# The query weights of a one-token attention block, loaded by eight transfers of sixteen partitions each

## The chip, the core and the metric

The kernel runs on one core of a Trainium2 chip. Its time is the device time of one execution in microseconds; the figure for the kernel before is the median of three runs. The core has five engines with instruction streams of their own: TensorE (PE; PEld is its weight load), VectorE (DVE), ScalarE (ACT), GpSimd (POOL) and SyncE (SP). SP does no arithmetic here: it issues DMA transfers, and sixteen DMA engines carry them out. Data lie in HBM (outside the core) and in SBUF, the core's own buffer of 128 partitions. TensorE adds up into PSUM.

## The reference

One token for each of two sequences is normalised, projected to 32 query heads, attends to a cache of 32768 keys and values for each of 8 key heads, and is projected back. The result is multiplied by the SiLU of a small gated MLP of the token itself and added to the token. All numbers are float32.

```
x, D = A_x, 512                                  # 2 x 1 x 512
xn = layernorm(x)
q = xn @ wq                                      # 512 x 4096: 32 heads of 128
scores = q . k_cache * 128**-0.5                 # k_cache 2 x 8 x 32768 x 128, 4 query heads share one
o = softmax(scores) . v_cache
s = o @ wo                                       # 4096 x 512
gate = x @ W_gate ; gate = gate * (gate > 0)     # 512 x 1792, as W_up
g = silu((gate * (x @ W_up)) @ W_down)
out = x + s * g
```

## The kernel before

**What is loaded.** The two caches are 256 MiB each (2 x 8 x 32768 x 128 x 4 bytes), the query weights `wq` 8 MiB, `wo` 8 MiB, the three MLP matrices 3.5 MiB each. Every byte is read once, so the kernel is above all a stream of DMA transfers.

**Buffers.** There are three large tiles in SBUF, each 128 partitions by 16384 floats (64 KiB a partition, 8 MiB in all): two for keys (`k0`, `k1`, in Python `kbuf`) and one, `wide` (shown as `w` in the profile), which holds first `wq`, then the gate and up weights, then the down weights, and then the values, a load at a time. The output weights `wo` go into `k1` at the end.

**How a load is written.** Every helper call records an operation with the tiles that it reads and writes; a small planner (`Program`) turns these into semaphore waits. `load(dst, src, sem, w=[...])` records one DMA on SP's queue whose completion adds 16 to the semaphore `sem`. The row of `wide` with number p takes four whole rows of `wq`, which lie one behind the other in HBM: 64 KiB in one piece. The load of `wq` is the first thing that SP issues:

```
QW = wq.shape[1] // 2
wqt = wide.rearrange("p (k h n) -> p k h n", k=NKC, h=2)
load(wide, wq.rearrange("(p k) n -> p (k n)", k=NKC), "wq", w=["wide"])
```

**The order of the work.** The order is that of the Python code; there is no scheduler. `load_kk(0)` (the first keys) follows the load of `wq` on SP. Then `project_q` multiplies the normalised token `xn`, which lies in `wt0`, by all of `wq` in 32 written matmuls (64 in the profile, since a float32 matmul is run in two passes). Its first matmul waits for the semaphore `wq`, that is, for the whole of `wq`, and for DVE's copy of `xn`:

```
for half in range(2):
    pe(chain([mm(pq[half][32 * c : 32 * c + 32, :], xn[:, k, :],
                 wqt[:, k, half, c * 512 : (c + 1) * 512], k == 0, k == NKC - 1)
              for k in range(NKC) for c in range(4)]),
       ["wt0", "wide"], [f"m{half}"])
```

`load_gu` overwrites `wide` with the gate and up weights, so SP waits for these matmuls before it issues it, and `load_kk(1)` stands behind that on SP. After this the 64 tiles of the caches (8192 tokens each) are worked through in pairs, in a loop `for j in range(PAIRS + 2)`: DVE turns the keys of a pair in 32 x 32 blocks (`k_transpose`, line 660 of the profile), TensorE makes the scores (`s`), DVE takes them out and keeps their maximum, ACT takes the exponential once a group of four tiles is complete, TensorE lays the weights out again (`pt`), DVE turns them (`wt`), and TensorE multiplies them by the values (`o`). SP issues the load of a pair's values into `wide` as soon as TensorE has finished with the values before, and the load of the next keys right behind it. The token itself, `x`, comes by two small transfers on ACT's queue, and DVE and ACT make `xn` of it while `wq` is on its way.

The profile gives the line 243 for every matmul recorded by the helper `mm`, and 240 for every transfer recorded by `load`.

Of the kernel before, what the change touches and what calls it, by code (L numbers as in the profile page):

```python
# [8 lines left out]
P = 128  # L9
# [6 lines left out]
ALIGN = 512  # L16
PERIOD = 4
APART = 16


class Op:
# [141 lines left out]
def decode_block_kernel(nc, x, kc, vc, wq, wo, wg, wu, wd, out):  # L163
# [8 lines left out]
    NKC = D // P  # L172
# [8 lines left out]
    def sbuf(name, *shape, align=32):  # L181
        return nc.alloc_sbuf_tensor(name, list(shape), F32, align_bytes=align)[:]
# [5 lines left out]
    wide = sbuf("w", P, 2 * NC * NR * DH, align=ALIGN)  # L188
# [41 lines left out]
    def dve(fn, r=(), w=()):  # L230
        pg.op("DVE", fn, r, w)
# [4 lines left out]
    def pe(fn, r=(), w=()):  # L236
        pg.op("PE", fn, r, w)

    def load(dst, src, sem, r=(), w=(), engine="SP"):
        pg.op(engine, lambda e: e.dma_start(dst, src), r, w, dma=sem)  # L240

    def mm(out_, lhs, rhs, start, stop):
        return lambda e: e.matmul(out_, lhs, rhs, start=start, stop=stop, skip_group_check=True)  # L243

    def chain(parts):
        def emit(e):
            for f in parts:
                got = f(e)
            return got

        return emit
# [6 lines left out]

    QW = wq.shape[1] // 2
    wqt = wide.rearrange("p (k h n) -> p k h n", k=NKC, h=2)  # L260
    load(wide, wq.rearrange("(p k) n -> p (k n)", k=NKC), "wq", w=["wide"])

    def of_columns(t):
        return t[0:P:APART, :]

    def by_column(t):
        return t.rearrange("b s (c n) -> c (b s) n", c=4)
# [20 lines left out]
    dve(lambda e: e.memset(xy, 0.0), w=["xy"])  # L288
    load(xp[0 : B * APART : APART, :], x.rearrange("b s d -> (b s) d"), "xp", w=["st0"], engine="ACT")
    load(of_columns(xy), by_column(x), "xy", w=["xy"], engine="ACT")  # L290
# [6 lines left out]
    for kb in range(4):  # L297
        dve(
            lambda e, kb=kb: e.memset(block_of[Q * kb : Q * kb + Q, kb * REP : (kb + 1) * REP], 1.0),
            w=["block_of"],  # L300
# [27 lines left out]
    n = 1  # L328
    while n < Q:
# [18 lines left out]
    dve(  # L348
        lambda e: e.tensor_copy(both, ident.rearrange("p (c k) -> p k c", c=NC)[:, 0 : B * APART : APART, :]),
        ["ident"],  # L350
# [40 lines left out]
                lambda e, k=k: e.transpose(  # L391
                    px[:, k * 32 : (k + 1) * 32], xquad[:, k, :], ident[:32, :32]
                )
# [62 lines left out]
    def project_q():  # L456
        pq = ps_m
        for half in range(2):
            pe(
                chain(  # L460
                    [
                        mm(
                            pq[half][32 * c : 32 * c + 32, :],
                            xn[:, k, :],
                            wqt[:, k, half, c * 512 : (c + 1) * 512],
                            k == 0,
                            k == NKC - 1,
                        )
                        for k in range(NKC)
                        for c in range(4)  # L470
                    ]
                ),
                ["wt0", "wide"],
                [f"m{half}"],
            )
        pt = ps_p[0]
        nq = REP * B * HKV
        turned = pt[:, :nq].rearrange("p (h b k) -> p h b k", h=REP, b=B)
        for half in range(2):
            qs = os_[half]  # L480
            dve(lambda e, q=qs, h=half: e.tensor_copy(q, pq[h]), [f"m{half}"], [f"os{half}"])  # L481
            pe(
                chain(
                    [
                        mm(
                            turned[:, h, :, half * NC : (half + 1) * NC],
                            qs[:, h * DH : (h + 1) * DH],
                            both,
                            True,
                            True,  # L490
                        )
                        for h in range(REP)
                    ]
                ),
                [f"os{half}", "both"],
                ["pt0"],
            )
        dve(lambda e: e.tensor_copy(qd.rearrange("p h b k -> p (h b k)"), pt[:, :nq]), ["pt0"], ["qd"])
        pq2 = ps_p[1]
        pe(  # L500
            chain(
                [
                    mm(
                        pq2[:, i * nq : (i + 1) * nq],
                        spread[:, i].rearrange("p k l -> p (k l)"),
                        qd.rearrange("p h b k -> p (h b k)"),
                        True,
                        True,
                    )
                    for i in range(4)  # L510
                ]
            ),
            ["st3", "qd"],
            ["pt1"],
        )
        dve(
            lambda e: e.tensor_copy(
                qall.rearrange("p b k e h -> p (b k) e h"),
                pq2[:, : 4 * nq].rearrange("p (e h g) -> p g e h", e=4, h=REP),
            ),  # L520
            ["pt1"],
            ["qall"],
        )
        take_query(0)

    def take_query(g):
        b, hk = group(g)
        pg.op(
            "POOL",
            lambda e: e.tensor_tensor(  # L530
                qcur.rearrange("p e (k h) -> p e k h", h=REP),
                qall[:, b, hk].unsqueeze(2).to_broadcast([P, 4, Q // REP, REP]),
                block_of.rearrange("p (k h) -> p k h", h=REP)
                .unsqueeze(1)
                .to_broadcast([P, 4, Q // REP, REP]),
                op=ALU.mult,
            ),
            ["qall", "block_of"],
            ["qcur", "pool"],
        )  # L540
# [243 lines left out]
    def finish_group(g):  # L784
# [27 lines left out]
            lambda e: e.tensor_copy(  # L812
                ots[mine, hk // 4, :, b * APART],
                ot[mine].rearrange("p (j m) -> p j m", j=ROWS)[:, :, 0],
# [61 lines left out]

    load_kk(0)
    project_q()
    load_gu()
    load_kk(1)  # L880
# [115 lines left out]
```

## Time and profile before

| | |
|---|---|
| time, median of 3 runs | 1309.93 us (1309.86 to 1310.05) |
| the profiled execution's own time | 1310.29 us |
| its span, first to last instruction | 1308.4 us |
| mean granted TensorE clock | 0.828 |
| PE busy | 859.0 us (66% of the span) |
| DVE busy | 718.1 us (55%) |
| ACT busy | 51.4 us (4%) |
| POOL busy | 10.5 us (1%) |
| SP's DMA queue, share of 16 DMA engines | 99.7% |
| read from HBM | 564.67 MB, 432 GB/s over the span |

The profile is of one execution, 0.36 us above the median of the runs. A busy share tells how long an engine had something under way; which engine sets the end is read from who waits for whom. Times in the answers are counted from the start of the span.

### The profile page before, as it was taken

What the parts mean: (1) busy time and instruction counts of PE and PEld (TensorE: products, weight loads), DVE (VectorE), ACT (ScalarE), POOL (GpSimd) and SP (SyncE); (2) the same over time, 40 slices, a digit from 0 to 9 for tenths busy, and PEclk for the clock granted to TensorE, in tenths of its full rate; (3) what the DMA queues carried; (4) which work ended last, traced back from release to release, by engine and by line L of the source; (5) the groups of instructions that cost most, each with busy time, mean ns of one, the idle gap of its engine ahead of it and who ended that gap; (6) DMA issues with size and microseconds to landing.
All of it is one profiled execution on the core that took longest, in us unless ns stands there. A gap on an engine that the chain in (4) does not pass through costs nothing.

```text
span 1308.4 us, 11146 instructions
## 1 busy us (share of the span) xinstructions
PE 859.0 (66%) x4720; PEld 211.5 (16%) x4720; DVE 718.1 (55%) x690; ACT 51.4 (4%) x133; POOL 10.5 (1%) x38
## 2 busy tenths in 40 slices
PE   3566675785666587576667667667665757865676
PEld 1111111211111121111111112121111112111121
DVE  3566654565655456664546666455665545656521
ACT  0001000000000000000000000000000000000000
POOL 0000000000000000000000000000000000000000
PEclk9677788878878887878898778798887889788788
DMA  9999999999999999999999999999999999999998
GB/s 417 423 438 435 437 431 441 425 439 429 437 429 439 435 433 441 429 441 427 439 429 437 429 439 435 433 441 429 441 427 439 429 437 429 439 435 433 439 431 357
DMA packets 10693, 564.79 MB, mean 432 GB/s; under 512 B 1195, under 2 KB 1211, under 8 KB 1597
## 3 DMA queue, kind: packets, MB, share of 16 engines
q1 hardware_dynamic: 10668, 564.67, 99.7%
q8 instruction: 6, 0.10, 0.0%
q14 instruction: 3, 0.02, 0.0%
q10 hardware_dynamic: 16, 0.01, 0.0%
HBM read 564.67 MB, written 0.00 MB: 432 GB/s over the span
## 4 chain that ended last, share of the span: by engine, by line
DMA 64%; DVE 17%; PE 15%; issue 4%; SPq 0%
DMA k<-in_A_k_cache_dram 58%; DVE k L660 17%; PE o L243 8%; PE s L243 6%; DMA k<-in_A_wo_dram 3%; DMA w<-in_A_wq_dram 2%; PE m_ps L243 1%; PE m_ps L693 0%; PE d L243 0%; SPq L240 0%; DVE gy L870 0%; DVE gy L872 0%
## 5 line engine op out<-in xcount | busy, mean ns | idle before, releaser
L243 PE MATMUL s<-k,qcur 128*32 128x512 f32 x2048 | 504.5, 710 | 370.5 <-DVE k L660 370.3
L660 DVE STREAM_TRANSPOSE k<-k 128x2048 f32<-128x2048 f32 x256 | 565.2, 2275 | 147.0 <-DMA k<-in_A_k_cache_dram 147.0
L243 PE MATMUL o<-w,wt 128*16 128x512 f32 x1984 | 245.5, 596 | 9.0 <-DMA w<-in_A_v_cache_dram 9.0
L243 PEld LDWEIGHTS s<-k,qcur 128*32 128x32 f32 x2048 | 89.5, 123 | 785.0 <-DVE k L660 639.3
L737 DVE STREAM_TRANSPOSE wt<-pt 128x512 f32<-128x512 f32 x64 | 45.9, 717 | 139.4 <-PE pt L243 134.6
L678 DVE TENSOR_SCALAR_CACHE_REDUCE st<-s 128x512 f32<-128x512 f32 x64 | 43.0, 672 | 120.9 <-PE s L243 120.9
L243 PEld LDWEIGHTS o<-w,wt 128*16 128x16 f32 x1984 | 62.4, 98 | 167.5 <-issue 167.5
L722 ACT ACTIVATE st<-st,nb 128x512 f32<-128x512 f32 x64 | 45.4, 710 | 1111.0 <-DVE nb L719 1111.0
L243 PE MATMUL pt<-st,perm 128*128 128x512 f32 x128 | 72.6, 696 | 1.5 <-ACT st L722 1.5
L763 DVE RECIPROCAL rl<-m_ps 128x1 f32<-128x1 f32 x16 | 2.7, 169 | 111.0 <-PE m_ps L243 111.0
L243 PE MATMUL m_ps<-ob,heads 128*128 128x128 f32 x128 | 21.7, 321 | 29.0 <-DVE ob L777 29.0
L243 PEld LDWEIGHTS pt<-st,perm 128*128 128x128 f32 x128 | 25.3, 219 | 34.4 <-issue 30.1
L803 DVE STREAM_TRANSPOSE os<-m_ps 128x512 f32<-128x512 f32 x16 | 11.5, 717 | 23.2 <-PE m_ps L243 23.2
L243 PEld LDWEIGHTS m_ps<-ob,heads 128*128 128x128 f32 x128 | 18.0, 217 | 31.1 <-DVE ob L777 31.1
L243 PE MATMUL m_ps<-w,wt 128*32 128x512 f32 (+1 forms) x128 | 16.2, 640 | 8.1 <-DMA w<-in_A_wq_dram 8.1
L777 DVE SCALAR_TENSOR_TENSOR ob<-o,share,ob 128x128 f32<-128x128 f32 x48 | 16.9, 351 | 1.7
L530 POOL TENSOR_TENSOR qcur<-qall,block_of 128x128 f32<-128x128 f32 x16 | 6.5, 406 | 1008.3 <-PE s L243 974.0
L243 PE MATMUL m_ps<-negone,mrow 1*128 1x1 f32 x32 | 6.0, 256 | 9.3 <-DVE mrow L708 9.3
L722 ACT ACTIVATION_READ_ACCUMULATOR st<-st,nb 128x1 f32 x64 | 11.9, 186 | 0.0
L481 DVE COPY os<-m_ps 128x512 f32<-128x512 f32 x2 | 1.4, 692 | 16.3 <-PE m_ps L243 16.3
L243 PE MATMUL o<-k,wt 128*16 128x512 f32 x64 | 8.4, 687 | 2.8 <-DMA k<-in_A_v_cache_dram 2.8
L391 PE MATMUL m_ps<-ident,st 32*128 32x32 f32 x4 | 0.7, 307 | 14.0 <-DVE st L380 14.0
(80 smaller groups left out, 102.8 us busy)
## 6 DMA issues: line engine op xcount, KB each, us to landing
k<-in_A_wo_dram SPq DMA_DIRECT2D x1, 4096.0 KB, 37.3
w<-in_B_W_gate_dram SPq DMA_DIRECT2D x1, 3584.0 KB, 19.6
w<-in_B_W_up_dram SPq DMA_DIRECT2D x1, 3584.0 KB, 27.6
w<-in_B_W_down_dram SPq DMA_DIRECT2D x1, 3584.0 KB, 15.6
k<-in_A_wo_dram SPq DMA_DIRECT2D x1, 2048.0 KB, 41.7
k<-in_A_wo_dram SPq DMA_DIRECT2D x1, 1024.0 KB, 43.7
k<-in_A_k_cache_dram SPq DMA_DIRECT2D x32, 48.2
k<-in_A_wo_dram SPq DMA_DIRECT2D x1, 512.0 KB, 44.5
```

What stands on the lines that cost most here:

```text
L243: return lambda e: e.matmul(out_, lhs, rhs, start=start, stop=stop, skip_group_check=True)
L391: lambda e, k=k: e.transpose(px[:, k * 32 : (k + 1) * 32], xquad[:, k, :], ident[:32, :32])
L481: dve(lambda e, q=qs, h=half: e.tensor_copy(q, pq[h]), [f"m{half}"], [f"os{half}"])
L530: lambda e: e.tensor_tensor(qcur.rearrange("p e (k h) -> p e k h", h=REP), qall[:, b, hk].unsqueeze(2).to_broadcast([P, 4, Q // REP, REP]) ...
L660: dve(lambda e: e.transpose(at_, at_), [f"k{t // 2 % 2}"], [key])
L678: lambda e: e.tensor_scalar(st[u], ps_s[t % 2], SCALE, None, op0=ALU.mult, op1=ALU.max, accum_out=mx[:, u : u + 1],),
L722: lambda e, u=u: e.activation(st[u], st[u], AF.Exp, bias=nb, scale=1.0, accum_out=ls[:, u : u + 1]),
L737: dve(lambda e: e.transpose(wt[t % 2], ps_p[t % 2]), [f"pt{t % 2}"], [f"wt{t % 2}"])
L763: dve(lambda e: e.reciprocal(rl, ps_m[1][:, :1]), ["m1"], ["rl"])
L777: lambda e, part=part, c=c: e.scalar_tensor_tensor(ob, part, share[:, c : c + 1], ob, op0=ALU.mult, op1=ALU.add),
L803: lambda e: e.transpose(ot, ps_m[1].rearrange("p (h q j) -> p j h q", h=REP, j=ROWS)),
```

## The change

The one transfer of `wq` is replaced by eight. Transfer i takes the partitions i, i + 8, i + 16 and so on up to i + 120, sixteen of them, and the rows of `wq` that belong to them: 16 x 64 KiB = 1 MiB. All eight add to the same semaphore `wq`, on which `project_q` now waits for 8 x 16 = 128 in place of 16. Each has a name of its own for what it writes, so that the planner puts no wait between them, and `project_q` lists these names as read. Nothing else differs: the same bytes come from the same places in HBM and go to the same places in SBUF.

```
+FIRST = 8
...
-    load(wide, wq.rearrange("(p k) n -> p (k n)", k=NKC), "wq", w=["wide"])
+    wq_rows = wq.rearrange("(p k) n -> p (k n)", k=NKC)
+    for i in range(FIRST):
+        load(wide[i:P:FIRST], wq_rows[i:P:FIRST], "wq", w=["wide" if i == 0 else f"wide_{i}"])
...
-                ["wt0", "wide"],
+                ["wt0", "wide", *(f"wide_{i}" for i in range(1, FIRST))],
                 [f"m{half}"],
```

On SP, at the start of the program, the order was this (`w` is the tile `wide`, `k` the key buffers; the shape is that of the destination, in partitions and floats):

```order
0 L943 UNCONDITIONAL_BRANCH
1 L240 DMA w<-in_A_wq_dram 128x16384
2 L240 DMA k<-in_A_k_cache_dram 128x16384
3 L240 DMA w<-in_B_W_gate_dram 128x7168
4 L240 DMA w<-in_B_W_up_dram 128x7168
5 L240 DMA k<-in_A_k_cache_dram 128x16384
```

In the changed kernel the same place of SP's stream reads:

```order
0 L946 UNCONDITIONAL_BRANCH
1 L241 DMA w<-in_A_wq_dram 16x16384 x8
2 L241 DMA k<-in_A_k_cache_dram 128x16384
3 L241 DMA w<-in_B_W_gate_dram 128x7168
4 L241 DMA w<-in_B_W_up_dram 128x7168
5 L241 DMA k<-in_A_k_cache_dram 128x16384
```

Seven instructions more stand ahead of the first load of keys; no instruction of another engine is added, removed or put elsewhere.

## The prediction

> **What bounds the kernel now.** I read the page first: its second part, which cuts the span into 40 slices, and its third, the DMA queues.
>
> ```profile
> span 1308.4 us, 11146 instructions
> DMA  9999999999999999999999999999999999999998
> GB/s 417 423 438 435 437 431 441 425 439 429 437 429 439 435 433 441 429 441 427 439 429 437 429 439 435 433 441 429 441 427 439 429 437 429 439 435 433 439 431 357
> q1 hardware_dynamic: 10668, 564.67, 99.7%
> ```
>
> The DMA engines are busy in every slice, and q1, SP's queue, holds all sixteen for 99.7% of the span. So the kernel is one stream of bytes. An engine of the core can finish earlier without moving the end, but a microsecond that the stream loses anywhere is lost, unless it ran dry elsewhere. How regular the stream is, the DMA view of the long middle stretch (100 to 1200 us) shows:
>
> ```profile
> DMA packets 8206, 477.82 MB, mean 434 GB/s; under 512 B 912, under 2 KB 912, under 8 KB 912
> q1 hardware_dynamic: 8202, 477.76, 100.2%
> ```
>
> The columns of the second line are packets, MB, and the share of sixteen engines. One engine moves 477.76 MB / (16 x 1100 us x 1.002) = 27.09 GB/s; a row of 64 KiB (65536 bytes) takes it 65536 / 27090 = 2.42 us. `wq` is 128 such rows, eight for each engine: 8 x 2.42 = 19.36 us.
>
> The start, from the timeline and the list of DMA issues (the last column of the issue is the time from issue to landing):
>
> ```profile
> 0.74 0.39 SPq L240 DMA_DIRECT2D w<-in_A_wq_dram  x1
> 1.19 0.41 SPq L240 DMA_DIRECT2D k<-in_A_k_cache_dram  x1
> 22.77 9.20 PE L243 MATMUL m_ps<-w,wt 128*32 128x512 f32 x64 [8.10 <-DMA w<-in_A_wq_dram]
> 32.03 0.33 SPq L240 DMA_DIRECT2D w<-in_B_W_gate_dram  x1
> 43.31 17.66 DVE L660 STREAM_TRANSPOSE k<-k 128x2048 f32<-128x2048 f32 x8 [7.57 <-DMA k<-in_A_k_cache_dram]
> 72.39 0.33 SPq L240 DMA_DIRECT2D w<-in_B_W_down_dram  x1
> 79.54 17.67 DVE L660 STREAM_TRANSPOSE k<-k 128x2048 f32<-128x2048 f32 x8 [4.36 <-DMA k<-in_A_k_cache_dram]
> w<-in_A_wq_dram SPq DMA_DIRECT2D x1, 21.9
> ```
>
> `wq` is issued at 0.74 and has landed 21.9 later, at 22.64: 19.36 us of moving and 2.54 us around it. The projection follows at once; when it has ended, SP issues the gate weights at 32.03. The first keys, queued since 1.19, are wanted by DVE and land just before 43.31, so at 32.03 the stream still has about 10 us of keys to move: it doesn't run dry. The down weights are issued at 72.39, some 7 us before the second keys land at 79.54.
>
> **What the change does, step by step.**
>
> *The issues.* Seven more transfers stand ahead of the first keys on SP. The nearest row is that of the six `wo` loads, which SP issues back to back:
>
> ```profile
> 1258.25 2.81 SPq L240 DMA_DIRECT2D k<-in_A_wo_dram  x6
> ```
>
> That is 2.81 / 6 = 0.47 us each. The keys are issued 7 x 0.47 = 3.3 us later, at 4.5. They queue behind 19 us of `wq`, so this costs nothing. With an eighth of the rows an engine's first row takes 2.42 us, and the next transfer is queued 0.47 us after the first: no engine waits for an issue.
>
> *The completions.* Seven more transfers end. Whether each pays a landing time in the stream, the `wo` loads tell, queued the same way:
>
> ```profile
> k<-in_A_wo_dram SPq DMA_DIRECT2D x1, 1024.0 KB, 43.7
> k<-in_A_wo_dram SPq DMA_DIRECT2D x1, 512.0 KB, 44.5
> ```
>
> They were issued 0.47 us apart and landed 0.47 + 44.5 - 43.7 = 1.27 us apart; 512 KiB (0.524 MB) at 434 GB/s take 1.21. A further transfer in the queue costs 0.06 us, so seven cost 0.4 us at most, and I put them at 0. [...]
>
> *The start of the first rows.* Between the issue and the landing lie 2.54 us that are not moving. A transfer with an eighth of the rows may hand out its first rows sooner. The gain lies between 0 and 1.0 us (from 0.74 to a start that leaves 1.5 us for the landing); I take 0.
>
> *Which rows are under way together.* This is what decides. Every transfer now has sixteen rows for sixteen engines: one row each, and all sixteen go to partitions eight apart. Before, an engine had eight rows of one transfer, in an order that the trace doesn't tell. In every long stretch of the trace all engines run at the same 27.1 GB/s, whatever the compute engines do:
>
> ```profile
> 0.00:22.64 22.64, 0.68 (x4) 0.55 (x4) 8.93 (x37) 2.86 (x3) 0.70 (x6) 1.00 0.99 417
> 100.00:1200.00 1100.00, 732.97 (x3921) 176.18 (x3919) 628.08 (x574) 45.58 (x122) 8.95 (x29) 0.83 1.00 434
> ```
>
> (The last two columns are the DMA share and GB/s.) PE is busy 3% of the first stretch and 67% of the second, and the DMA share is full in both, the first one's 417 holding the start. That is a fixed width, filled to the end, somewhere between HBM and the partitions, and the transfers of 128 partitions fill it: nothing is left to gain. If the width is that of sixteen ways *into the partitions*, then sixteen rows keep the rate only where they meet each way once. Eight apart over the whole buffer, they are either one on each way or, at the next even spread, two on each of eight ways. In the second case both take turns, a row takes 2 x 2.42 = 4.84 us, and `wq` takes 8 x 4.84 = 38.7 us: 19.36 more. The bounds of this term are 0 (each way once) and 19.36 (two on each). I take the upper end, since a rearrangement of a full stream can only keep its rate or lose, and keeping it needs the special case.
>
> [...]
>
> *What waits behind it.* `wq` lands 19.36 us later, at 42.0. The token's own chain is on its way meanwhile:
>
> ```profile
> 10.13 0.68 DVE L364 TENSOR_REDUCE stat<-st 32x1 f32<-32x512 f32 x1 [2.91 <-DMA st<-in_A_x_dram]
> 14.71 0.29 DVE L401 COPY wt<-m_ps 128x128 f32<-128x128 f32 x1 [0.78 <-PE m_ps L391]
> ```
>
> `x` lands among the rows of `wq`; with rows twice as long it lands by 2 x 10.13 = 20.3, and `xn` is there 4.87 us later, at 25.1, before 42.0. It costs nothing. The projection moves by 19.36, and so do the gate weights' issue (51.4) and the end of the first keys (62.7), which an engine takes up when its eight rows of `wq` are done. The margins of 10 and 7 us stay as they are, so the whole program behind moves by the same 19.36 us, no less: the stream has no idle time in which to make it up.
>
> **The sum.** Issues 0, completions 0, first rows 0, rows two on a way 19.36. The profiled execution took 1310.29 us, which gives 1329.65; against the median of the runs, 0.36 us lower, 1309.93 + 19.36 = **1329.3 us**, slower by 1.5%.
>
> **The rivals.** I call a difference under 0.2% (2.6 us) no change, about what a measurement of this kernel can tell.
>
> *Not slower: the width is that of the sending engines.* If each DMA engine itself moves 27.1 GB/s and the partitions take whatever comes, a row stays at 2.42 us, `wq` at 19.36, and only the start changes, by 0 to -1.0 us: 1309.4 us. For it speaks that sixteen engines at one rate look the same either way; against it, that the change would then need sixteen equal ways of more than the engine's width, of which the trace shows no sign. It decides if a 64 KiB row of `wq` stays under 2.7 us: above that the extra of 8 rows passes 2.6 us.
>
> *The engine follows the partition.* If a row's engine is chosen by the way it goes to, each transfer gives eight engines two rows and the other eight none. [...] The trace of before can't speak of it.
>
> [...]
>
> *Paid one after the other.* Should the eight transfers follow each other with a gap, seven gaps of up to 2.54 us (the part of `wq`'s 21.9 that isn't moving) add 17.8 us: 1327.7 us. The `wo` rows speak against it with 0.06.
>
> *Faster than the bound* asks for 2.6 us, more than all that the issue and landing of `wq` take together (2.54); only a loss elsewhere in the stream that happens to vanish could add to it, and the share of 99.7% leaves 3.9 us for that.
>
> **How the numbers follow.** Two on each way: 0.74. Uneven sharing: 0.08. Gaps: 0.02. Engines as the width: 0.10. Engine by partition: 0.04. Faster than the bound: 0.02. This gives slower 0.84, within 0.2% 0.14, faster 0.02. The forecast's own range is one row (2.42 us) to either side, for rows that overlap at the turn from one half of the ways to the other and for a margin that is used up: 1326.9 to 1331.7. To hold the time 8 times in 10 it reaches up to 1332 and down to 1318, past the uneven pair's 1319.6; left out are the cases near 1310, 0.16 together.
>
> **What would show it.** In the profile after, eight issues of `wq` back to back within 4 us on SP; in the stretch until `wq` lands about 210 GB/s in place of 417; the projection's first matmul at about 42 in place of 22.77; the first keys' transposes at about 62.7; and from there every stage as long as before, at 434 GB/s. [...] A total that grows by clearly more or less than the projection's start moves would refute the last step, that nothing is made up or lost behind it.

## The result and the profile after

The changed kernel takes 1331.24 us (median of six runs, 1331.02 to 1331.45) against 1309.99 us for the kernel before (six runs, 1309.86 to 1311.05): 21.25 us more, a ratio of 1.0162 with a 95% interval of 1.0151 to 1.0173. The forecast was 1329.3 us, 1.9 us less.

The page of the profile after shows where it is. First its span, the rates of its 40 slices and SP's queue:

```profile
span 1329.5 us, 11153 instructions
GB/s 221 339 433 445 436 438 422 440 434 440 426 436 434 440 426 436 436 436 434 430 436 438 440 422 440 434 440 424 440 432 440 428 436 434 438 430 434 436 436 359
q1 hardware_dynamic: 10780, 564.67, 99.7%
```

The loss stands in the first slice and part of the second (a slice is 33 us), 221 and 339 GB/s in place of 417 and 423. From the third on the rates are the old ones. The queue is as busy as before, 99.7%: the DMA engines never stand still, they move less. The stages, by windows (columns as before; the last two are the DMA share and GB/s):

```profile
0.00:44.31 44.31, 0.68 (x4) 0.58 (x5) 8.93 (x37) 2.86 (x3) 0.70 (x6) 1.00 0.98 213
44.31:64.48 20.17, 11.78 (x88) 5.31 (x88) 2.03 (x4) 0.00 (x0) 0.41 (x1) 0.84 0.95 410
100.00:1200.00 1100.00, 736.72 (x3969) 177.83 (x3970) 631.32 (x567) 42.65 (x114) 8.75 (x28) 0.83 1.00 434
```

Until the projection starts, the engines move 213 GB/s, half of the 417 before, and 434 in the long middle stretch, as before. The timeline at the places shown of before:

```profile
0.74 5.04 SPq L241 DMA_DIRECT2D w<-in_A_wq_dram  x8
5.82 0.58 SPq L241 DMA_DIRECT2D k<-in_A_k_cache_dram  x1
44.31 8.79 PE L244 MATMUL m_ps<-w,wt 128*32 128x512 f32 x64 [25.95 <-DMA w<-in_A_wq_dram]
53.16 0.33 SPq L241 DMA_DIRECT2D w<-in_B_W_gate_dram  x1
64.48 2.31 DVE L663 STREAM_TRANSPOSE k<-k 128x2048 f32<-128x2048 f32 x1 [7.62 <-DMA k<-in_A_k_cache_dram]
```

The projection starts 21.54 us later (44.31 for 22.77), the first keys are turned 21.17 us later (64.48 for 43.31), and the span is 21.1 us longer: nearly all that the load of `wq` lost comes out at the end.

How long a row of 64 KiB takes is read from GB/s divided by the DMA share, which is what sixteen busy engines move. The DMA view of the stretch from 5 to 40 us, all of it `wq`:

```profile
DMA packets 240, 7.35 MB, mean 210 GB/s; under 512 B 118, under 2 KB 126, under 8 KB 128
q1 hardware_dynamic: 224, 7.34, 102.0%
```

210 / 1.02 = 206 GB/s for sixteen engines, 12.9 for one, so a row takes 65536 bytes / 12.87 GB/s = 5.09 us in place of 2.42. At this pace eight rows take 40.7 in place of 19.4, 21.4 us more. The trace also records every packet by itself, with its start, its duration and its size; a packet here is a row, 65536 bytes, or the piece of a row that one transfer carries. By these records the first sixteen rows of `wq` took 4.38 to 5.33 us, after 2.68 to 3.36 before, and all later ones 4.91 to 5.15, after 2.42.

### The profile page after: what moved, and what is told of

Same layout as the page of the kernel before. It is cut to its first block, busy times and chain, and to the rows that moved or that the text cites. A ratio compares the mean times of both kernels' runs of the same rounds, so it can differ in the third digit from the quotient of the medians.

```text
span 1329.5 us, 11153 instructions
## 1 busy us (share of the span) xinstructions
PE 856.5 (64%) x4720; PEld 212.6 (16%) x4720; DVE 718.0 (54%) x690; ACT 51.4 (4%) x133; POOL 10.5 (1%) x38
## 3 DMA queue, kind: packets, MB, share of 16 engines
q1 hardware_dynamic: 10780, 564.67, 99.7%
## 4 chain that ended last, share of the span: by engine, by line
DMA 64%; DVE 18%; PE 14%; issue 4%; SPq 0%
DMA k<-in_A_k_cache_dram 58%; DVE k L663 18%; PE o L244 8%; PE s L244 5%; DMA k<-in_A_wo_dram 3%; DMA w<-in_A_wq_dram 3%; PE m_ps L244 1%; SPq L241 0%; PE m_ps L696 0%; DVE gy L873 0%; DVE gy L875 0%
## 5 line engine op out<-in xcount | busy, mean ns | idle before, releaser
L244 PE MATMUL s<-k,qcur 128*32 128x512 f32 x2048 | 497.9, 696 | 372.1 <-DVE k L663 371.9
L244 PE MATMUL pt<-st,perm 128*128 128x512 f32 x128 | 76.9, 732 | 1.5 <-ACT st L725 1.5
L244 PEld LDWEIGHTS m_ps<-w,wt 128*32 128x32 f32 x128 | 5.9, 120 | 34.4 <-issue 34.4
```

## The experiments

The theory is that of the forecast, called "ways" here: the partitions are reached by sixteen ways, and a transfer loses when its rows meet on fewer. It is a theory: no record shows a way, or which partitions share one; what the runs show is rates. Against it stood that a transfer of sixteen rows, or the number of transfers, costs by itself; that the rows read together lie badly in HBM; and that an engine follows the partition. All times are set against the kernel before on the same chip, 1309.87 to 1309.99 us. Each edit is of the loop that loads `wq` in the changed kernel; `FIRST` is always the number of transfers.

**Sixteen neighbours.**

```
-        load(wide[i:P:FIRST], wq_rows[i:P:FIRST], ...)
+        load(wide[16 * i : 16 * i + 16], wq_rows[16 * i : 16 * i + 16], ...)
```

> wq by eight transfers of 16 neighbouring partitions each (0 to 15, 16 to 31, ...). [...] Number of transfers (each transfer with one row per engine costs by itself what the eighth of 21.3 us is): the same +21 as with every eighth partition. Engine chosen by partition: no row waits for another, +0 to +3.

Measured: 1364.85 us, +54.9, ratio 1.0417 (1.0387 to 1.0447). The DMA view from 12 to 70 us, all `wq`:

```profile
DMA packets 208, 6.30 MB, mean 109 GB/s; under 512 B 102, under 2 KB 110, under 8 KB 112
q1 hardware_dynamic: 192, 6.29, 97.0%
```

109 / 0.97 = 112 GB/s, 9.3 us a row: close to four times 2.42. The same number of transfers, of the same size, costs 2.6 times as much (54.9 for 21.25), so the number of transfers by itself is not the cause, and an engine that follows the partition is refuted too.

**Eight transfers by columns.**

```
-        load(wide[i:P:FIRST], wq_rows[i:P:FIRST], ...)
+        cut = slice(2048 * i, 2048 * i + 2048)
+        load(wide[:, cut], wq_rows[:, cut], ...)
```

> wq by eight transfers of 1 MiB, each to all 128 partitions and an eighth of the columns (8 KiB a row). Ways: all rows keep ways of their own, +0 to +1 us over the kernel before. Number of transfers: eight transfers of the same size as in the changed kernel, +21 us, or +7 x 2.54 = +17.8 if only the part that is not moving counts.

Measured: 1309.92 us, -0.07, ratio 0.9998 (0.9987 to 1.0009), no change. The projection starts where it did:

```profile
22.82 9.07 PE L244 MATMUL m_ps<-w,wt 128*32 128x512 f32 x64 [11.15 <-DMA w<-in_A_wq_dram]
```

Eight transfers of 1 MiB cost nothing if each goes to all 128 partitions.

**Another place in HBM.**

```
-        load(wide[i:P:FIRST], wq_rows[i:P:FIRST], ...)
+        load(wide[i:P:FIRST], wq_rows[16 * i : 16 * i + 16], ...)
```

> As the changed kernel, transfer i to the partitions i, i + 8, ..., but with the 16 neighbouring rows 16 i to 16 i + 15 of the weights as its source, so that the rows read together lie 64 KiB apart in HBM in place of 512 KiB. The weights stand in other partitions than the reference has them, so the query is computed from reordered weights; the work is the same. Ways into the partitions: +21 us as the changed kernel. Conflict of the reads in HBM: near the kernel before, +0 to +3.

Measured: 1331.37 us, +21.4, ratio 1.0162 (1.0132 to 1.0191), as the changed kernel. With the source changed and the destination kept, the loss stays: it is on the side of the partitions.

**Two transfers of 64, and four of 32.**

```
-FIRST = 8
+FIRST = 2
```

> wq by two transfers, of the even and of the odd partitions, 64 each, four rows for an engine. All sixteen ways are reached by each transfer. Ways, met at the same time, with an engine's rows neighbours in the transfer: at any time the sixteen rows are eight partitions apart again, two on a way: +21 us. If what counts is which ways the whole transfer reaches: +0 to +1. Number of transfers: one more than before, +2.7.

Measured: 1310.77 us, +0.8, ratio 1.0006 (0.9995 to 1.0017), which can't be told from no change: the window from 5 to 20 us shows 464 / 1.07 = 434 GB/s, which in the words of the theory is all sixteen ways. The +21 of the order that I had put first, an engine's rows neighbours in the transfer, did not come. With `FIRST = 4`:

> wq by four transfers to every fourth partition, 32 rows each, two rows for an engine. [...] (b) An engine gets two neighbours of the transfer: the rows under way together are eight partitions apart as in the changed kernel, +21 us.

Measured: 1310.48 us, +0.5, ratio 1.0004 (0.9993 to 1.0016), no change. The +21 of two neighbours of the transfer for one engine (b) did not come either: the window from 5 to 20 us shows 459 / 1.06 = 433 GB/s.

**Two halves.** The counterpart with the same number of transfers and rows:

```
-FIRST = 8
+FIRST = 2
...
-        load(wide[i:P:FIRST], wq_rows[i:P:FIRST], ...)
+        load(wide[64 * i : 64 * i + 64], wq_rows[64 * i : 64 * i + 64], ...)
```

> wq by two transfers, of partitions 0 to 63 and of 64 to 127. The same number of transfers and of rows as with the even and the odd partitions, which cost +0.8. [...] If only the number of transfers or of rows in one counted: +0.8.

Measured: 1331.5 us, +21.55, ratio 1.0164 (1.0135 to 1.0194). Two transfers of 64 rows cost nothing or 21.5 us, by the partitions alone. The rate is that of the changed kernel, 5% under half of 434, which is 217: the window from 5 to 40 us shows 210 / 1.02 = 206 GB/s.

```profile
5.00:40.00 35.00, 0.69 (x4) 0.55 (x4) 5.61 (x21) 1.58 (x2) 0.00 (x0) 1.00 1.02 210
```

**Sixteen rows, four partitions apart.**

```
-    for i in range(FIRST):
-        load(wide[i:P:FIRST], wq_rows[i:P:FIRST], ...)
+    parts = [slice(32 + j, 96, 4) for j in range(4)] + [slice(0, 32), slice(96, P)]
+    for i, part in enumerate(parts):
+        load(wide[part], wq_rows[part], ...)
```

> [...] Ways: the first four transfers (4 MiB) run at the full rate, 2.42 us a row and about 430 GB/s for the first 10 us, though each is a transfer of sixteen rows of 64 KiB as in the changed kernel; a cost of sixteen-row transfers would give 210 GB/s there. [...]

Measured: 1320.94 us, +11.0, ratio 1.0084 (1.0054 to 1.0113). Windows of the first four transfers and of the two tails:

```profile
5.00:12.00 7.00, 0.00 (x0) 0.00 (x0) 4.94 (x20) 0.60 (x2) 0.00 (x0) 1.00 1.04 451
14.00:30.00 16.00, 0.00 (x0) 0.00 (x0) 0.00 (x0) 0.00 (x0) 0.00 (x0) 1.00 0.95 197
```

451 / 1.04 = 434 GB/s with transfers of sixteen rows: the full rate. This is the closest counterpart to the changed kernel, with the same size of transfer and one row for an engine, and these four transfers lose nothing. The tails, 32 neighbours each, run at 197 / 0.95 = 207, the rate of every eighth partition. Four rows of an engine at 5.09 in place of 2.42 are 10.7 us, the 11.0 measured; at 9.3 us a row, the pace of sixteen neighbours, they would be 4 x (9.3 - 2.42) = 27.5.

**The loss twice.** The first load of keys is split in the same way:

```
+        if j == 0:
+            for i in range(FIRST):
+                load(kbuf[0][i:P:FIRST], rows_of(kc, 0)[i:P:FIRST], "k0",
+                     w=k_keys(0) if i == 0 else [f"k0_part{i}"])
+            return
```

> As the changed kernel, and the first load of keys (also 128 rows of 64 KiB) is split in the same way into eight transfers to every eighth partition; the compute waits for all eight. Ways, and nothing made up behind it: twice the cost, +42.5 us over the kernel before. If part of the loss is hidden by work that waits for something else, clearly less than twice.

Measured: 1352.93 us, +43.0, ratio 1.0328 (1.0298 to 1.0358). Twice 21.25 is 42.5, within the spread of this kernel's two runs (1352.27 and 1353.6): no sign that anything behind the loads makes up for it.

**Rows seven apart.** Here the theory gives no number, since no run shows which of these partitions share a way.

```
-        load(wide[i:P:FIRST], wq_rows[i:P:FIRST], ...)
+        part = slice(i, 112, 7) if i < 7 else slice(112, P)
+        load(wide[part], wq_rows[part], ...)
```

> wq by eight transfers of 16 rows: seven of them take every seventh partition (i, i + 7, ..., i + 105), the eighth the partitions 112 to 127. [...] Two rows on a way whatever the partitions (a cost of transfers of sixteen rows): +21. Ways of eight neighbouring partitions each: mostly one row on each of fourteen, and the eighth transfer with eight on each of two, far above +20.

Measured: 1331.42 us, +21.45, ratio 1.0164 (1.0134 to 1.0193), as much as every eighth partition. That is the +21 of a cost of transfers of sixteen rows, but four such transfers, with rows four apart, had run at 434 GB/s. Ways of eight neighbouring partitions each, far above +20, do not fit. The next run puts one set of rows seven apart, the one from partition 11, ahead of the others, in four pieces of 16 KiB a row:

```
+    cut = [slice(4096 * n, 4096 * n + 4096) for n in range(4)]
+    parts = [(slice(11, 117, 7), c) for c in cut]
+    parts += [(slice(s, s + 106, 7), slice(0, 16384)) for s in range(12, 18)]
+    parts += [(slice(0, 11), slice(0, 16384)), (slice(123, P), slice(0, 16384))]
```

> [...]

Measured: 1340.44 us, +30.5, ratio 1.0232 (1.0203 to 1.0262). The records of the single packets tell more than a window of 2 us. A piece of 16 KiB at the full rate takes 2.42 / 4 = 0.61 us. Of the 23 pieces of the first set that start from 2.8 to 4.1 us, sixteen take 0.61 to 0.63 and seven 0.70 to 0.93; of the 26 that start later, fourteen take 0.66 to 1.47. So rows of such a set can run at the full rate, but the set is not free of loss. Why the whole load loses 30.5 us, more than every eighth partition, no run shows.

**The sets from 15 and from 13.** The last two runs put another set of rows seven apart first, from partition 15 in the one and from 13 in the other, and the set from 11 behind it, each in two pieces of 32 KiB a row:

```
+    cut = [slice(8192 * n, 8192 * n + 8192) for n in range(2)]
+    parts = [(slice(s, s + 106, 7), c) for s in (15, 11) for c in cut]     # the other run: (13, 11)
```

> [...] A row of 32 KiB alone takes 1.21 us. [...]

> [...]

The window from 4 to 6 us, with the second pieces, of the run with the set from 15 and then of that with the set from 13:

```profile
4.00:6.00 2.00, 0.00 (x0) 0.00 (x0) 1.83 (x9) 0.70 (x1) 0.00 (x0) 1.00 1.29 412
```

```profile
4.00:6.00 2.00, 0.00 (x0) 0.00 (x0) 1.83 (x9) 0.70 (x1) 0.00 (x0) 1.00 1.03 229
```

Divided by the share, these are 412 / 1.29 = 319 GB/s against 229 / 1.03 = 222. A window of 2 us counts whole packets by their start and holds pieces of the next set too, so the single packets tell more. Fourteen of the sixteen second pieces of the set from 15 take 1.21 to 1.23 us, the time at the full rate, and two take 2.91 and 3.18. Of the set from 13 all sixteen take 2.02 to 2.51. In the same run the second pieces of the set from 11 take 1.21 to 1.40, fourteen of them 1.21 to 1.23: the full rate. The whole times, one run each (1338.74 and 1338.86 us), are those of a mixture of sets and say nothing of this.

So sets of the same size and spacing differ by where they start: two slow rows from 15, sixteen from 13. Two slow rows look like a pair that meets, an estimate from their number alone; sixteen do not. The sets under way beside them may count as well: in the run with rows seven apart, the rows of the sets that start at 3 and at 4 took 2.94 to 4.79 us in place of 2.42, and there rows of neighbouring sets were under way together. But in the run before these, the set from 11 had slow pieces from 4.17 us on, 1.3 us before the first row of another set started; so neighbouring sets need not be the only reason. What holds up these rows stays open; which engine moves which row is not in the records.

## Why the prediction was right

**The direction and the place.** The stream of bytes was full, a full stream that is rearranged can only keep its rate or lose, and the changed kernel moved at half the rate in the first 44 us (213 GB/s for 417). That the cause is the destination, and not the number of transfers, the size, or HBM, is shown by three pairs: the even and odd partitions against the halves (+0.8 and +21.55), the columns against every eighth partition (-0.07 and +21.25), and the source changed under the same destination (+21.4).

**Rows two on a way** had nearly the right size and came out too small. That the rows meet two by two was a choice between two spreads: no trace of before has a transfer to every eighth partition, and no run shows the ways themselves. What the runs showed in its place is the rate: 206 GB/s to every eighth partition and to each half of the buffer, 434 to every second partition. I let two rows share what one engine moves alone, 4.84 us a row; it was 5.09. Counted as eight ways, an estimate from the rate, 206 / 8 = 25.7 GB/s pass on each, less than the 27.1 of one engine before. The sum also took all eight rows of before at 2.42, though the first one was slower. In the packets' records the eight rows of an engine took 40.4 us on average, after 20.0 before: 20.4 us more, where the forecast had 19.36. This is 1.0 of the 1.9 us by which the forecast was short. The time still fell into the range of one row to either side (up to 1331.7), but that range was given for other reasons, so this is in part luck. No run shows its turn from one half of the ways to the other: after the first sixteen, every row of `wq` took 4.91 to 5.15 us.

**The cost of issues** was mis-sized, harmlessly: 5.04 / 8 = 0.63 us each in place of 0.47, so the keys were issued at 5.82 and not at 4.5. They still queued behind `wq`.

**The completions** at nothing held for eight transfers to all partitions, which cost -0.07 us. In the changed kernel 1.5 us pass between the mean end of the engines' last rows of `wq` and the projection, after 0.8 before. These 0.7 us were put at nothing; part of them is that the engines end further apart (42.12 to 43.27, after 21.66 to 22.30), the rest is not explained.

**The first rows** came no sooner but 0.4 us later, at 2.15 after 1.76 in the packets' records, outside the gain of 0 to 1.0 that I had allowed. With 20.4 and 0.7 this makes up the 21.54 us at the projection. The 1.5 us for the landing in the bound of that gain was assumed; before, 0.8 us passed from the mean end of the last rows to the projection.

**What waits behind** held: `xn` was ready well before `wq`, as these rows of the profile after show, at 18.68 and not as late as the 25.1 that I had allowed:

```profile
13.81 0.68 DVE L367 TENSOR_REDUCE stat<-st 32x1 f32<-32x512 f32 x1 [6.61 <-DMA st<-in_A_x_dram]
18.39 0.29 DVE L404 COPY wt<-m_ps 128x128 f32<-128x128 f32 x1 [0.78 <-PE m_ps L394]
```

That the whole program moves by the loss held to 0.4 us (21.54 at the projection, 21.1 in the span, 21.25 in the time), and splitting a second load doubled it.

**The rivals.** The engines as the width: rows would have stayed under 2.7 us (2.42 + 2.6 / 8 is 2.75, to be exact); they took 5.09. Engine by partition: refuted by sixteen neighbours, +54.9 us where +0 to +3 was expected. Uneven pairs: of two rows that meet, one would have gone first at 2.42 us, and no row of `wq` took less than 4.38; the 1319.6 us named for them rest on an order of the ways that no run shows. Gaps between transfers: the DMA share stayed at 1.02, full.

The prediction argued with the sixteen rows under way at one moment. The runs show that for even sets of partitions the whole transfer's partitions set the rate, with few or many rows: 433 to 434 GB/s with 16 rows four apart, 32 four apart, 64 two apart, or all 128; 206 to 207 with 16 rows eight apart, or 32 or 64 neighbours; 112 with 16 neighbours, tried with 16 alone. In the words of the theory these are sixteen, eight and four ways, an estimate from the rates. For uneven sets, such as rows seven apart, the runs give no such count.

## What to carry to other kernels

With the DMA engines busy 99.7% of the span, splitting a load cost nothing that could be told here when it was cut by columns (-0.07 us), or into every second or every fourth of the 128 partitions (+0.8 and +0.5). Every eighth partition spreads evenly over the buffer too and moved only 206 GB/s of 434 (+21.25). Rows seven apart lost 21.45 us, and no count here tells which of their sets lose. A DMA share of 100% doesn't show such a loss, it was 102% in the changed kernel's load; GB/s divided by the share does, with 206.

## What the runs showed of the hardware beyond this

Sixteen neighbours move 112 GB/s, more than half of the 206 of every eighth partition. Counted as four and eight ways, an estimate from these rates, that is 28 a way with four rows on it and 25.7 with two, against 27.1 with one. And rows seven apart show no single rate: of the set from 13 all sixteen pieces took 2.02 to 2.51 us in place of 1.21, while of the set from 15 fourteen took 1.21 to 1.23 and two 2.91 and 3.18, and a load of such sets lost 21.45 us. No run here tells what couples these rows.
